# Reordering the opening of a fused attention and MLP kernel: first loads, small tables, first sixteenths, second chunk

## Chip, cores and metric

One core of a Trainium2 chip runs the kernel. The metric is the device time of one execution in microseconds (us). The engines have queues of their own and work in the order of their queues: PE (TensorE: matrix products; its weight loads are shown as PEld), DVE (VectorE), ACT (ScalarE), POOL (GpSimd) and SP (SyncE, which here only issues DMAs).

## The reference

Linear attention with decay over 4 batches, 8 heads, 768 positions and head size 64, in blocks of 64 with a carried state; then an MLP with a snake activation over the 3072 tokens.

```python
for b in range(nb):                       # blocks of 64 positions
    intra = np.einsum('bhic,bhjc->bhij', qb, kb) * Dmask[None]     # lam ** (i - j), i >= j
    intra = np.einsum('bhij,bhjd->bhid', intra, vb)
    inter = np.einsum('bhid,bhde->bhie', qb * lam_pow[None], kv_state)
    out[:, :, sl] = intra + inter
    kv_state = lam_block * kv_state + np.einsum('bhsd,bhse->bhde', kb * rev_pow, vb)
x = out.transpose(0, 2, 1, 3).reshape(B * S, H * D)                # 3072 x 512
h = x @ w_in                                                       # w_in 512 x 2048
g = h + np.sin(alpha * h) ** 2 / (alpha + 1e-09)
return g @ w_out                                                   # w_out 2048 x 512
```

Inputs and output are float32; the products run in bfloat16.

## The kernel before

The positions are cut into six chunks of 128. A chunk's attention over the four batches gives one group g of 512 tokens (128 of each batch), held as `xt[g]`: 128 partitions x 4 parts of the model dimension x 512 tokens, where batch b fills columns 128 b to 128 b + 127. A unit u = 4 t + b is batch b of chunk t.

The MLP goes by groups. Its hidden dimension of 2048 is cut into sixteen columns of 128, the sixteenths f. `hidden(g, f)` does four products of 512 columns on PE (line 400), then ACT takes the Sin (403) and, for most f, the Square (406); `finish(g, f)` on DVE adds that to h (413; for even f below 8 in group 0 it also squares, 412). `project(g, n)` does a quarter of an output tile (428). The order on every engine is written by hand: the loop at line 597 runs group g, and in its sixteenth i it places `hidden(g, i)`, the attention of chunk g + 1 as listed by `slots(g)` (541), a projection, `finish(g, i)`, and from `feed(g)` (574) the work of POOL and SP. PE, ACT and DVE each take their part of that list in that order.

Attention of one unit in chunks 0 and 1: `transposes` (221, 224) turns k and q on PE with an identity into one bank of PSUM, ACT copies the result (227, QKT); `scores` (235) makes the products of k and q in the bank `pf`, DVE multiplies them by the decay mask `Cmask` (243, STm); `intra_mm` (283) and `inter_mm` (291) make the output, `copy_x` (297) writes it to `xt`. In chunk 0 there is no carried state, and `first_out` (466, 470) does the output. `part_fo(uf, uo)` does the output of unit uo and the scores of uf in between. `part_k` (254, 261) makes the sums of the state, `state_put` (269) and `state_decay` (275) put them in place on POOL. Chunks 2 to 5 go by pairs of batches, with other tables (`NEp`, `Rpair`, `trip`, made in `tables_of_pairs`) and DMA transposes on SP.

Banks of PSUM go by tags: `pf`, `po`, `pqk`, `ops`, `h0`, `h1`, `h2` hold one thing at a time. The first nine sixteenths of group 0 take the banks of `FIRST`, later ones h0, h1, h2 in turn. The transposes of chunk 1's units use pqk, po, pqk, ops; the first projection needs ops.

Loads: k and q of batch 0 in chunk 0 come over SP's queue as float32 (`kraw`, `qraw`) and are cast by DVE (451, 458). Everything else is issued by POOL (line 100; chunks 2 on also at 96; w_in at 106, w_out at 110), which casts to bfloat16 on the way, in the order written: k and q of batch 1, v of batch 0, the rest of chunk 0, w_in in five pieces, chunk 1 in halves of two batches. The kdec products of POOL (214) stand among the last of these.

The opening (479 to 520) is chunk 0's attention, ahead of group 0. `spin(n)` puts n products without use on PE, as filling; `pcol` holds -1 - p, 127 - p and, in columns 2 and 3, the exponents of the pair tables, each made by iota on POOL; `pos_row` holds 1 to 128 in every row. `iden` and `idf` are identities made by POOL, `tri` the triangle of the mask.

Of the kernel before, what the change touches and what calls it, by code (L numbers as in the profile page):

```python
# [7 lines left out]

ALU = mybir.AluOpType
ACTF = mybir.ActivationFunctionType  # L10
FP32 = mybir.dt.float32
BF16 = mybir.dt.bfloat16
# [3 lines left out]
def kernel(  # L16
# [11 lines left out]
    nc = tc.nc  # L28
    P = nc.NUM_PARTITIONS

    B, H, S, D = q.shape
    T = 128
    NT = S // T
    HP = H // 2
    DM, DFF = moe_w_in.shape
    NDC = DM // P
# [40 lines left out]
    def new_chunk(t):  # L77
        for d, nm in ((qn, "qn"), (kn, "kn"), (vn, "vn")):
            d[t] = qkvp.tile([P, B, H, D], BF16, name=nm)
# [8 lines left out]
    def load(t, i, b0, b1):  # L88
        dst, src = KQV[i]
        if i != 1 and t >= 2:  # L90


            for c in range(b0 // 2, b1 // 2):
                for n in range(2):
                    t0 = t * T + c * D
                    nc.gpsimd.dma_start(  # L96
                        out=dst[t][n * D:(n + 1) * D, 2 * c:2 * c + 2, :, :].rearrange("p b h e -> p (b h) e"),
                        in_=src[2 * n:2 * n + 2, :, t0:t0 + D, :].rearrange("b h p e -> p (b h) e"))
            return
        nc.gpsimd.dma_start(  # L100
            out=dst[t][:, b0:b1, :, :].rearrange("p b h e -> p (b h) e"),
            in_=src[b0:b1, :, t * T:(t + 1) * T, :].rearrange("b h p e -> p (b h) e"))
# [6 lines left out]
    def load_w_out(i):  # L109
# [1 line left out]
                            in_=moe_w_out[i * 512:(i + 1) * 512, :].rearrange("(f p) d -> p f d", p=P))  # L111


    pcol = consts.tile([P, 4], FP32, name="pcol")
    nc.gpsimd.iota(out=pcol[:, 0:1], pattern=[[0, 1]], base=-1, channel_multiplier=-1,
                   allow_small_or_imprecise_dtypes=True)
    nc.gpsimd.iota(out=pcol[:, 1:2], pattern=[[0, 1]], base=T - 1, channel_multiplier=-1,
                   allow_small_or_imprecise_dtypes=True)
    new_chunk(0)
    load(0, 0, 1, 2)  # L120
    load(0, 1, 1, 2)
    iden = consts.tile([P, P], BF16, name="iden")
    make_identity(nc, iden[:])
    fill = consts.tile([P, 512], BF16, name="fill")
    nc.vector.memset(fill[:], 1.0)  # L125
    tri = consts.tile([P, T], FP32, name="tri")
    nc.vector.memset(tri[:], 1.0)
    nc.gpsimd.affine_select(out=tri[:], in_=tri[:], pattern=[[1, T]], compare_op=ALU.is_ge,
                            fill=0.0, base=0, channel_multiplier=-1)
    pos_row = consts.tile([P, T], FP32, name="pos_row")  # L130
    nc.gpsimd.iota(out=pos_row[:], pattern=[[1, T]], base=1, channel_multiplier=0,
                   allow_small_or_imprecise_dtypes=True)
    load(0, 2, 0, 1)
    for b in range(2, B):
        for i, bi in ((0, b), (1, b), (2, b - 1)):
            load(0, i, bi, bi + 1)
    load(0, 2, B - 1, B)
    for r in range(2):
        for c in range(2):
            nc.gpsimd.iota(out=pcol[r * D:(r + 1) * D, 2 + c:3 + c], pattern=[[0, 1]], base=-1 - D * c,  # L140
                           channel_multiplier=-1, allow_small_or_imprecise_dtypes=True)
    idf = consts.tile([NFC, NFC], FP32, name="idf")
    make_identity(nc, idf[:])
    for i in range(4):
        load_w_in(i)
    new_chunk(1)
    load(1, 0, 0, 2)
    load(1, 1, 0, 2)
    load_w_in(4)

    kv = [consts.tile([P, HP, 2, D], BF16, name=f"kv{b}") for b in range(B)]
    for b in range(B):
        nc.vector.memset(kv[b][:], 0.0)


    lnlam = consts.tile([P, H], FP32, name="lnlam")
# [17 lines left out]
    Cmask1 = consts.tile([P, 2, HP, D], FP32, name="Cmask1")  # L174
    Rpair = consts.tile([P, 2, H], FP32, name="Rpair")

    def powers_of_pairs():
        for c in range(2):
            nc.scalar.activation(out=NEp[:, c], in_=lnlam[:].rearrange("p (hp hd) -> p hd hp", hd=2),
                                 func=ACTF.Exp, scale=pcol[:, 2 + c:3 + c])  # L180

    def tables_of_pairs():

        lo, hi = slice(0, D), slice(D, P)
        nc.sync.dma_start(out=Rpair[hi, 0, :], in_=Rtok[lo, :])
        nc.sync.dma_start(out=Rpair[lo, 1, :], in_=Rtok[hi, :])
        nc.gpsimd.tensor_copy(out=Rpair[lo, 0, :], in_=Rtok[lo, :])
        nc.gpsimd.tensor_copy(out=Rpair[hi, 1, :], in_=Rtok[hi, :])
        nc.gpsimd.tensor_copy(out=trip[lo, :], in_=tri[lo, :])
        nc.gpsimd.memset(trip[hi, :], 1.0)  # L190
        nc.gpsimd.affine_select(out=trip[hi, :], in_=trip[hi, :], pattern=[[1, T]], compare_op=ALU.is_ge,
                                fill=0.0, base=0, channel_multiplier=-1)
        for c, C in enumerate((Cmask, Cmask1)):
            n = T - D * c
            nc.gpsimd.tensor_tensor(out=C[:], in0=trip[:, 0:n].unsqueeze(1).unsqueeze(1).broadcast_to([P, 2, HP, n]),
                                    in1=NEp[:, c].unsqueeze(3).broadcast_to([P, 2, HP, n]), op=ALU.mult)
# [195 lines left out]
    def h_tag(g, f):  # L392
        return f"h{(g * NFC + f) % 3}"

    def hidden(g, f):

        tag = FIRST[f] if g == 0 and f < len(FIRST) else h_tag(g, f)
        hps = psA.tile([P, GRP], FP32, name="hps", tag=tag)
        for c in range(NDC):
            nc.tensor.matmul(out=hps[:], lhsT=w_in_of[f][:, c, :],  # L400
                             rhs=xt[g][:, c, :], start=(c == 0), stop=(c == NDC - 1))
        s_sb = mlps.tile([P, GRP], BF16, name="s_sb")
        nc.scalar.activation(out=s_sb[:], in_=hps[:], func=ACTF.Sin, scale=alpha_sb[:, f:f + 1])  # L403
        s2 = mlps.tile([P, GRP], BF16, name="s2")
        if on_act(g, f):
            nc.scalar.activation(out=s2[:], in_=s_sb[:], func=ACTF.Square)  # L406
        hps_of[g, f] = (hps, s_sb, s2)
# [68 lines left out]
        for _ in range(n):  # L476
            nc.tensor.matmul(out=ps[:, 0:cols], lhsT=fill[:, 0:P], rhs=fill[:, 0:cols], start=True, stop=True)  # L477

    spin(9)
    for nm, src, tag in (("KT", kn, "pqk"), ("QT", qn, "ops")):  # L480
        X_ps = psA.tile([P, HP, T], BF16, name="X_ps", tag=tag)
        for hp in range(HP):
            nc.tensor.transpose(out=X_ps[:, hp, :], in_=src[0][:, 0, 2 * hp:2 * hp + 2, :], identity=iden[:])
        XT = firstp.tile([P, HP, T], BF16, name=nm)
        nc.scalar.copy(out=XT[:], in_=X_ps[:])
        st[0][nm] = XT[:]
        spin(3)
    scores(0)
    spin(1)
    transposes(1, "pqk")  # L490
    for hp in range(HP):
        nc.scalar.activation(out=Etab[:, hp, :], in_=pos_row[:], func=ACTF.Exp, scale=ln_hd[:, hp:hp + 1])
    spin(2)
    transposes(2, "ops")
    powers_of_pairs()
    warm = consts.tile([P, 1], FP32, name="warm")
    nc.scalar.activation(out=warm[:], in_=lnlam[:, 0:1], func=ACTF.Sin)
    spin(1)
    scores(1)
    spin(1)  # L500
    first_out(0, "po")
    spin(1)
    scores(2)
    a_ps = psA.tile([P, NFC], FP32, name="a_ps", tag="h2")
    nc.tensor.transpose(out=a_ps[:], in_=alpha_fp[:], identity=idf[:])
    transposes(3, "pqk")
    spin(2)
    first_out(1, "h1")
    alpha_sb = consts.tile([P, NFC], FP32, name="alpha_sb")
    nc.vector.tensor_copy(out=alpha_sb[:], in_=a_ps[:])  # L510
    r_sb = consts.tile([P, NFC], FP32, name="r_sb")
    nc.vector.reciprocal(out=r_sb[:], in_=alpha_sb[:])
    spin(2)
    scores(3, 2)
    spin(1)
    first_out(2, "po")
    spin(2)
    first_out(3, "h1", range(0, 2))
    first_out(3, "ops", range(2, 4))
    spin(3)  # L520


    def part_fo(uf, uo, bank="po"):
# [15 lines left out]
    def slots(g):  # L539

        u = [B * (g + 1) + b for b in range(B)]
        T_, FO = transposes, part_fo
        if g == 0:
            return {}, {3: [(part_k, (0, 1), "pf")], 6: [(part_k, (2, 3), "pf")],
                    7: [(T_, u[0])], 8: [(T_, u[1], "po")], 9: [(FO, u[0], None)],
                    11: [(FO, u[1], u[0]), (copy_x, u[0])], 12: [(T_, u[2])],
                    13: [(FO, None, u[1]), (T_, u[3], "ops"), (copy_x, u[1])], 14: [(FO, u[2], None)]}, {}

        p, q_ = (u[0], u[2]), (u[1], u[3])
        pre, at, post = {}, {}, {}  # L550
        if g == 1:
            at = {4: [(part_k, (4, 6), h_tag(1, 5))], 6: [(part_k, (5, 7), h_tag(1, 7))]}
        for us, s0, s1 in ((p, 9, 11), (q_, 13, 15)) if g == 1 else ((p, 5, 8), (q_, 10, 13)):

            early = g == 1 and us == q_
            scores_ = [(pair_scores, us, h_tag(g, s0 + 1))]
            out_ = [(pair_out, us, h_tag(g, s1 + 1) if g < NT - 2 else None), (sum_state, us[0]), (copy_x, us[0])]
            rest = [(copy_x, us[1]), (sum_state, us[1])]
            if early:
                pre[s0] = scores_ + [(pair_mask, us)]  # L560
                pre[s1] = out_ + rest
            else:
                at[s0], post[s0] = scores_, [(pair_mask, us)]
                at[s1], post[s1] = out_, rest
        return pre, at, post
# [102 lines left out]
```

## Time and profile before

| what | us |
|---|---|
| three runs | 215.27, 217.73, 215.68 |
| median | 215.68 |
| the profiled execution's own time | 217.63 |
| its span, first to last instruction | 215.70 |

| engine | busy us | share of the span |
|---|---|---|
| PE | 206.7 | 96% |
| ACT | 147.3 | 68% |
| DVE | 124.3 | 58% |
| POOL | 107.2 | 50% |

By place: the opening runs to 18.5 us, when group 0's first sixteenth starts on PE; sixteenth 15 of group 0 starts at 41.9, the first projection at 42.76, group 1 at 47.97. The matrix products of the MLP (lines 400 and 428) are on the chain of work that ended last for 71% of the span. The profile's page cuts the span into 40 slices; each digit is a share in tenths, and PEclk is the clock that PE was granted:

```profile
PE   7889986999999999999999999999999999999994
POOL 8999999896999799607479316210000000000000
PEclk9999999799999999999999999999999999999999
DMA  5999999999999999991995993990210101111022
```

A line of the timeline holds the start, the busy time, the engine, the line of the code, the operation with output and inputs, how many, and in brackets how long the engine had been idle and what ended that. Lines of several instructions have been merged, so that the busy time is that of all of them.

### The profile page before, as it was taken

The page shows a single profiled execution, that of the slowest core. Times are in us where ns is not written, and L with a number is a line of the kernel's source. Part 1 is how long each engine was busy: PE and PEld are TensorE (multiplying, and loading weights), DVE is VectorE, ACT ScalarE, POOL GpSimd, SP SyncE. Part 2 cuts the span into 40 slices and gives each one's busy share as a digit, 9 for nine tenths or more (in the row PEclk, how much of TensorE's full clock was granted, in tenths as well). Part 3 has the DMA queues.
Part 4 walks back from the last instruction along what each step waited for, and adds up shares of the span by engine and source line. Part 5 has one row for each costly group of instructions (what it writes and reads, how often), then busy time and mean ns, then how long its engine had stood idle before and what let it go on. Part 6 is the DMA issues. An engine that isn't in the chain of part 4 may idle for free.

```text
span 215.7 us, 4606 instructions
## 1 busy us (share of the span) xinstructions
PE 206.7 (96%) x1856; PEld 99.8 (46%) x1856; DVE 124.3 (58%) x191; ACT 147.3 (68%) x236; POOL 107.2 (50%) x155
## 2 busy tenths in 40 slices
PE   7889986999999999999999999999999999999994
PEld 2444443444444554454544454544454544444453
DVE  4576988472557784577664568654766644444300
ACT  5583897827776667975758785768767679788531
POOL 8999999896999799607479316210000000000000
PEclk9999999799999999999999999999999999999999
DMA  5999999999999999991995993990210101111022
GB/s 103 150 145 174 175 176 175 208 183 152 169 197 163 148 172 112 146 146 51 140 181 50 196 122 26 175 146 22 78 49 2 52 0 52 47 53 49 0 97 97
DMA packets 100214, 24.69 MB, mean 114 GB/s; under 512 B 92369, under 2 KB 97249, under 8 KB 100193
## 3 DMA queue, kind: packets, MB, share of 16 engines
q0 software_dynamic: 77280, 13.37, 80.3%
q1 hardware_dynamic: 22912, 11.03, 23.3%
q8 instruction: 14, 0.23, 0.5%
q14 instruction: 8, 0.06, 0.1%
HBM read 27.28 MB, written 6.29 MB: 156 GB/s over the span
## 4 chain that ended last, share of the span: by engine, by line
PE 81%; POOL 11%; DMA 5%; issue 1%; ACT 0%; POOLq 0%; ACTq 0%
PE ops L428 37%; PE hps L400 34%; DMA qn<-in_q_dram 5%; POOL vn L100 2%; POOL kn L100 2%; PE O_ps L371 2%; POOL kdec L214 2%; POOL qn L100 2%; POOL w_in L106 2%; PE hps L442 2%; PE O_ps L365 1%; PE F_ps L330 1%; PE KVA_ps L356 1%; PE O_ps L283 1%; PE O_ps L291 1%
## 5 line engine op out<-in xcount | busy, mean ns | idle before, releaser
L413 DVE SCALAR_TENSOR_TENSOR gall<-s,r_sb,hps 128x512 bf16<-128x512 bf16 x96 | 71.3, 746 | 62.1 <-ACT s L406 61.7
L400 PE MATMUL hps<-xt,w_in 128*128 128x512 bf16 x384 | 98.5, 382 | 0.1
L403 ACT ACTIVATE s_sb<-hps,alpha_sb 128x512 bf16<-128x512 f32 x96 | 65.8, 687 | 47.5 <-PE hps L400 47.5
L428 PE MATMUL ops<-w_out,gall 128*128 128x512 bf16 x368 | 93.1, 379 | 0.0
L406 ACT ACTIVATE s<-s_sb 128x512 bf16<-128x512 bf16 x92 | 57.9, 630 | 3.0
L400 PEld LDWEIGHTS <-w_in 128*128 128x128 bf16 x384 | 36.9, 98 | 44.7 <-issue 2.4
L428 PEld LDWEIGHTS <-gall 128*128 128x128 bf16 x368 | 34.9, 98 | 39.7
L269 POOL CAST kv<-kvs 64x256 bf16<-64x256 f32 x40 | 16.1, 402 | 30.4 <-PE O_ps L371 22.4
L297 DVE TENSOR_TENSOR xt<-O_ps,Etab 128x512 bf16<-128x512 f32 x20 | 13.7, 687 | 6.8 <-PE O_ps L291 3.5
L433 ACT COPY o_sb<-ops 128x512 f32<-128x512 f32 x23 | 13.1, 571 | 6.0 <-PE ops L428 6.0
L96 POOL DMA_DIRECT2D kn<-in_k_dram x16 | 13.3, 850 | 0.0
L96 POOL DMA_DIRECT2D vn<-in_v_dram x16 | 13.2, 845 | 0.0
L100 POOL DMA_DIRECT2D qn<-in_q_dram x10 | 12.8, 1278 | 0.7 <-DMA w_out<-in_moe_w_out_dram 0.7
L477 PE MATMUL hps<-fill 128*128 128x512 bf16 x31 | 10.9, 459 | 1.5 <-DVE fill L125 1.5
L306 POOL TENSOR_TENSOR kdec<-kn,Rpair 128x1024 bf16<-128x1024 bf16 x6 | 11.4, 1910 | 1.6 <-DMA kn<-in_k_dram 1.6
L243 DVE TENSOR_TENSOR STm<-F_ps,Cmask 128x1024 bf16<-128x1024 f32 (+1 forms) x9 | 9.8, 1095 | 3.5 <-PE F_ps L235 3.5
L275 POOL TENSOR_TENSOR kvd<-kvs,L 128x256 f32<-128x256 f32 x16 | 9.8, 615 | 1.0
L341 DVE TENSOR_TENSOR STm<-F_ps,Cmask 128x1024 bf16<-128x1024 f32 x8 | 9.7, 1217 | 0.0
L227 ACT COPY QKT<-QK_ps 128x1024 bf16<-128x1024 bf16 x7 | 7.0, 1004 | 2.7 <-PE QK_ps L224 2.7
L214 POOL TENSOR_TENSOR kdec<-kn,Rtok 128x512 bf16<-128x512 bf16 x8 | 8.5, 1106 | 0.1
L338 DVE TENSOR_TENSOR STm<-G_ps,Cmask 128x256 bf16<-128x256 f32 x16 | 6.0, 419 | 0.6
L100 POOL DMA_DIRECT2D vn<-in_v_dram x6 | 6.0, 1012 | 0.0
(83 smaller groups left out, 116.1 us busy)
## 6 DMA issues: line engine op xcount, KB each, us to landing
out_dram<-o_sb SPq DMA_DIRECT2D x23, 256.0 KB, 2.2
vn<-in_v_dram POOLq DMA_DIRECT2D x20, 128.0 KB, 4.9
kn<-in_k_dram POOLq DMA_DIRECT2D x19, 128.0 KB, 5.8
w_out<-in_moe_w_out_dram POOLq DMA_DIRECT2D x4, 512.0 KB, 14.0
w_in<-in_moe_w_in_dram POOLq DMA_DIRECT2D x3, 512.0 KB, 9.8
qn<-in_q_dram POOLq DMA_DIRECT2D x3, 512.0 KB, 9.1
qn<-in_q_dram POOLq DMA_DIRECT2D x4, 256.0 KB, 11.7
w_in<-in_moe_w_in_dram POOLq DMA_DIRECT2D x2, 256.0 KB, 5.7
```

What stands on the lines that cost most here:

```text
L96: nc.gpsimd.dma_start(out=dst[t][n * D:(n + 1) * D, 2 * c:2 * c + 2, :, :].rearrange("p b h e -> p (b h) e"), in_=src[2 * n:2 * n + 2, :, ...
L100: nc.gpsimd.dma_start(out=dst[t][:, b0:b1, :, :].rearrange("p b h e -> p (b h) e"), in_=src[b0:b1, :, t * T:(t + 1) * T, :].rearrange("b h ...
L214: nc.gpsimd.tensor_tensor(out=kdec[:], in0=kn[t][:, b, :, :], in1=head_bc(Rtok), op=ALU.mult)
L269: nc.gpsimd.tensor_copy(out=kv[b][s, :, hd, :], in_=kvs[u][s, :, :])
L297: nc.vector.tensor_tensor(out=xt[t][:, :, b * T:(b + 1) * T], in0=st[u]["O_ps"], in1=Etab[:], op=ALU.mult)
L306: nc.gpsimd.tensor_tensor(out=kdec[:], in0=kn[t][:, b::2, :, :], in1=Rpair[:].unsqueeze(3).broadcast_to([P, 2, H, D]), op=ALU.mult)
L400: nc.tensor.matmul(out=hps[:], lhsT=w_in_of[f][:, c, :], rhs=xt[g][:, c, :], start=(c == 0), stop=(c == NDC - 1))
L403: nc.scalar.activation(out=s_sb[:], in_=hps[:], func=ACTF.Sin, scale=alpha_sb[:, f:f + 1])
L406: nc.scalar.activation(out=s2[:], in_=s_sb[:], func=ACTF.Square)
L413: nc.vector.scalar_tensor_tensor(out=gall[g][:, f, :], in0=s2[:], scalar=r_sb[:, f:f + 1], in1=hps[:], op0=ALU.mult, op1=ALU.add)
L428: nc.tensor.matmul(out=ops[:], lhsT=gall[g][:, f, m * P:(m + 1) * P], rhs=w_out_sb[part][:, f % 4, :], start=(f == 0), stop=(f == NFC - 1))
L433: nc.scalar.copy(out=o_sb[:], in_=ops[:])
```

## The change

- POOL issues the loads of k and q of batch 1 first, and the iotas `pcol` and `pos_row` follow. `pcol` keeps two columns; the four iotas of columns 2 and 3 go.
- `iden`, `tri` and `idf` are made by DVE from `pos_row` and `pcol`. The memsets of `kv` stand ahead of them in the code.
- `NEp`, which ACT made with two Exps, is put together of `NE`: one half by two DMAs on SP, the other by two copies on POOL. The DMAs of `Rpair` now stand at the top level, behind those.
- In the opening the order on PE changes: the transposes of batch 1 come ahead of scores 0, the alpha transpose and its reciprocal come early, scores 1 comes ahead of the transposes of batch 2, both outputs of batches 0 and 1 ahead of scores 2, and batch 3 is transposed in two halves (`half_T`) with a copy each. The Exps of `Etab` stand behind the copy of batch 1, the warming Sin behind scores 2.
- `hidden` can begin a sixteenth with the first 256 columns (batches 0 and 1) and do the other 256 later. The opening ends with such a beginning of sixteenths 0 and 1 of group 0.
- In group 0 the list of chunk 1's attention moves by one sixteenth: transposes of the four units in sixteenths 8, 9, 13, 14 in place of 7, 8, 12, 13, the rest with them. `feed` is as before.

```diff
+    new_chunk(0)
+    load(0, 0, 1, 2)
+    load(0, 1, 1, 2)
+    pcol = consts.tile([P, 2], FP32, name="pcol")
     nc.gpsimd.iota(out=pcol[:, 0:1], pattern=[[0, 1]], base=-1, channel_multiplier=-1,
...
+    nc.vector.tensor_scalar(out=iden[:], in0=pos_row[:], scalar1=pcol[:, 0:1], scalar2=0.0,
+                            op0=ALU.add, op1=ALU.is_equal)
     tri = consts.tile([P, T], FP32, name="tri")
+    nc.vector.tensor_scalar(out=tri[:], in0=pos_row[:], scalar1=pcol[:, 0:1], scalar2=0.0,
+                            op0=ALU.add, op1=ALU.is_ge)
+    idf = consts.tile([NFC, NFC], FP32, name="idf")
+    nc.vector.tensor_copy(out=idf[:], in_=iden[0:NFC, 0:NFC])
...
-    for r in range(2):
-        for c in range(2):
-            nc.gpsimd.iota(out=pcol[r * D:(r + 1) * D, 2 + c:3 + c], pattern=[[0, 1]], base=-1 - D * c,
-                           channel_multiplier=-1, allow_small_or_imprecise_dtypes=True)
-    idf = consts.tile([NFC, NFC], FP32, name="idf")
-    make_identity(nc, idf[:])
...
+    nc.sync.dma_start(out=NEp[hi, 0], in_=NE[lo])
+    nc.sync.dma_start(out=NEp[lo, 1], in_=NE[hi])
+    nc.sync.dma_start(out=Rpair[hi, 0, :], in_=Rtok[lo, :])
+    nc.sync.dma_start(out=Rpair[lo, 1, :], in_=Rtok[hi, :])
...
+        nc.gpsimd.tensor_copy(out=NEp[lo, 0], in_=NE[lo])
+        nc.gpsimd.tensor_copy(out=NEp[hi, 1], in_=NE[hi])
...
+    def hidden(g, f, start_only=False):
+        parts = [slice(0, GRP)]
+        if (g, f) in begun:
+            hps, parts = begun.pop((g, f)), [slice(GRP // 2, GRP)]
+        else:
+            hps = psA.tile([P, GRP], FP32, name="hps", tag=tag)
+        if start_only:
+            begun[g, f], parts = hps, [slice(0, GRP // 2)]
+        for w in parts:
+            for c in range(NDC):
+                nc.tensor.matmul(out=hps[:, w], lhsT=w_in_of[f][:, c, :],
+                                 rhs=xt[g][:, c, w], start=(c == 0), stop=(c == NDC - 1))
+        if start_only:
+            return
...
+    spin(9)
+    half_T(0, "KT", "pqk")
+    spin(3)
+    half_T(0, "QT", "ops")
+    spin(1)
+    transposes(1, "po")
+    spin(1)
     scores(0)
...
     spin(2)
+    scores(1)
+    spin(1)
+    transposes(2, "pqk")
+    spin(1)
+    first_out(0, "po")
+    spin(1)
+    first_out(1, "h1")
+    spin(1)
+    scores(2)
...
+    half_T(3, "KT", "ops")
+    spin(1)
+    half_T(3, "QT", "h2")
+    spin(1)
+    first_out(2, "po")
     scores(3, 2)
+    spin(3)
     first_out(3, "h1", range(0, 2))
     first_out(3, "ops", range(2, 4))
-    spin(3)
+    hidden(0, 0, True)
+    hidden(0, 1, True)
...
-                    7: [(T_, u[0])], 8: [(T_, u[1], "po")], 9: [(FO, u[0], None)],
-                    11: [(FO, u[1], u[0]), (copy_x, u[0])], 12: [(T_, u[2])],
-                    13: [(FO, None, u[1]), (T_, u[3], "ops"), (copy_x, u[1])], 14: [(FO, u[2], None)]}, {}
+                    8: [(T_, u[0])], 9: [(T_, u[1], "po")], 10: [(FO, u[0], None)],
+                    12: [(FO, u[1], u[0]), (copy_x, u[0])], 13: [(T_, u[2])],
+                    14: [(FO, None, u[1]), (T_, u[3], "ops"), (copy_x, u[1])], 15: [(FO, u[2], None)]}, {}
```

More of the change, by code (lines that the diff above doesn't have):

```diff
@@ L6 @@
 from concourse._compat import with_exitstack
-from concourse.masks import make_identity
 ALU = mybir.AluOpType
@@ L111, in load_w_out @@
                             in_=moe_w_out[i * 512:(i + 1) * 512, :].rearrange("(f p) d -> p f d", p=P))
-    pcol = consts.tile([P, 4], FP32, name="pcol")
+    new_chunk(0)
+    load(0, 0, 1, 2)
+    load(0, 1, 1, 2)
+    pcol = consts.tile([P, 2], FP32, name="pcol")
     nc.gpsimd.iota(out=pcol[:, 0:1], pattern=[[0, 1]], base=-1, channel_multiplier=-1,
+                   allow_small_or_imprecise_dtypes=True)
+    pos_row = consts.tile([P, T], FP32, name="pos_row")
+    nc.gpsimd.iota(out=pos_row[:], pattern=[[1, T]], base=1, channel_multiplier=0,
                    allow_small_or_imprecise_dtypes=True)
@@ L118 @@
                    allow_small_or_imprecise_dtypes=True)
[L119 to L123, printed above, removed]
     fill = consts.tile([P, 512], BF16, name="fill")
     nc.vector.memset(fill[:], 1.0)
-    tri = consts.tile([P, T], FP32, name="tri")
[L127 to L132, printed above, removed]
+    kv = [consts.tile([P, HP, 2, D], BF16, name=f"kv{b}") for b in range(B)]
+    for b in range(B):
+        nc.vector.memset(kv[b][:], 0.0)
+    iden = consts.tile([P, P], BF16, name="iden")
+    nc.vector.tensor_scalar(out=iden[:], in0=pos_row[:], scalar1=pcol[:, 0:1], scalar2=0.0,
+                            op0=ALU.add, op1=ALU.is_equal)
+    tri = consts.tile([P, T], FP32, name="tri")
+    nc.vector.tensor_scalar(out=tri[:], in0=pos_row[:], scalar1=pcol[:, 0:1], scalar2=0.0,
+                            op0=ALU.add, op1=ALU.is_ge)
+    idf = consts.tile([NFC, NFC], FP32, name="idf")
+    nc.vector.tensor_copy(out=idf[:], in_=iden[0:NFC, 0:NFC])
     load(0, 2, 0, 1)
@@ L149 @@
     load_w_in(4)
-    kv = [consts.tile([P, HP, 2, D], BF16, name=f"kv{b}") for b in range(B)]
-    for b in range(B):
-        nc.vector.memset(kv[b][:], 0.0)
     lnlam = consts.tile([P, H], FP32, name="lnlam")
@@ L175 @@
     Rpair = consts.tile([P, 2, H], FP32, name="Rpair")
[L177 to L180, printed above, removed]
+    lo, hi = slice(0, D), slice(D, P)
+    nc.sync.dma_start(out=NEp[hi, 0], in_=NE[lo])
+    nc.sync.dma_start(out=NEp[lo, 1], in_=NE[hi])
+    nc.sync.dma_start(out=Rpair[hi, 0, :], in_=Rtok[lo, :])
+    nc.sync.dma_start(out=Rpair[lo, 1, :], in_=Rtok[hi, :])
     def tables_of_pairs():
-        lo, hi = slice(0, D), slice(D, P)
-        nc.sync.dma_start(out=Rpair[hi, 0, :], in_=Rtok[lo, :])
-        nc.sync.dma_start(out=Rpair[lo, 1, :], in_=Rtok[hi, :])
+        nc.gpsimd.tensor_copy(out=NEp[lo, 0], in_=NE[lo])
+        nc.gpsimd.tensor_copy(out=NEp[hi, 1], in_=NE[hi])
         nc.gpsimd.tensor_copy(out=Rpair[lo, 0, :], in_=Rtok[lo, :])
@@ L393, in h_tag @@
         return f"h{(g * NFC + f) % 3}"
-    def hidden(g, f):
+    begun = {}
+    def hidden(g, f, start_only=False):
         tag = FIRST[f] if g == 0 and f < len(FIRST) else h_tag(g, f)
[L398 to L401, printed above, removed]
+        parts = [slice(0, GRP)]
[11 more added lines that the diff above has]
+            return
         s_sb = mlps.tile([P, GRP], BF16, name="s_sb")
@@ L477, in spin, with half_T @@
             nc.tensor.matmul(out=ps[:, 0:cols], lhsT=fill[:, 0:P], rhs=fill[:, 0:cols], start=True, stop=True)
-    spin(9)
-    for nm, src, tag in (("KT", kn, "pqk"), ("QT", qn, "ops")):
+    def half_T(u, nm, tag):
+        src = {"KT": kn, "QT": qn}[nm]
         X_ps = psA.tile([P, HP, T], BF16, name="X_ps", tag=tag)
         for hp in range(HP):
-            nc.tensor.transpose(out=X_ps[:, hp, :], in_=src[0][:, 0, 2 * hp:2 * hp + 2, :], identity=iden[:])
+            nc.tensor.transpose(out=X_ps[:, hp, :], in_=src[0][:, u, 2 * hp:2 * hp + 2, :], identity=iden[:])
         XT = firstp.tile([P, HP, T], BF16, name=nm)
         nc.scalar.copy(out=XT[:], in_=X_ps[:])
-        st[0][nm] = XT[:]
-        spin(3)
+        st[u][nm] = XT[:]
+    spin(9)
[5 more added lines that the diff above has]
+    spin(1)
     scores(0)
-    spin(1)
-    transposes(1, "pqk")
+    a_ps = psA.tile([P, NFC], FP32, name="a_ps", tag="h2")
+    nc.tensor.transpose(out=a_ps[:], in_=alpha_fp[:], identity=idf[:])
     for hp in range(HP):
         nc.scalar.activation(out=Etab[:, hp, :], in_=pos_row[:], func=ACTF.Exp, scale=ln_hd[:, hp:hp + 1])
[L493 to L508, printed above, removed]
     alpha_sb = consts.tile([P, NFC], FP32, name="alpha_sb")
@@ L513 @@
     spin(2)
-    scores(3, 2)
+    scores(1)
[7 more added lines that the diff above has]
+    scores(2)
+    warm = consts.tile([P, 1], FP32, name="warm")
+    nc.scalar.activation(out=warm[:], in_=lnlam[:, 0:1], func=ACTF.Sin)
+    spin(1)
+    half_T(3, "KT", "ops")
+    spin(1)
+    half_T(3, "QT", "h2")
     spin(1)
     first_out(2, "po")
-    spin(2)
+    scores(3, 2)
+    spin(3)
     first_out(3, "h1", range(0, 2))
     first_out(3, "ops", range(2, 4))
-    spin(3)
+    hidden(0, 0, True)
+    hidden(0, 1, True)
     def part_fo(uf, uo, bank="po"):
```

## The prediction

> **What bounds the kernel now.** I read the chain that ended last first: where the end is decided.
>
> ```profile
> 18.42 4.25 POOL kdec L214 x4
> 22.67 1.18 POOL vn L100
> 23.85 1.12 POOL kn L100
> 24.97 11.80 DMA qn<-in_q_dram
> 36.81 0.57 PE QK_ps L224 x4
> 37.38 1.71 PE hps L400 x4
> ```
>
> Columns: start, length, what. POOL's queue, full from 1.9 us, leads to the issue at 24.97 of q of chunk 1, batches 2 and 3. It lands 11.80 us later, at 36.77, and its transposes start at once. After that the chain is all but PE. Then PE's timeline around it:
>
> ```profile
> 33.41 1.02 PE L400 MATMUL hps<-xt,w_in 128*128 128x512 bf16 x4
> 35.09 0.40 PE L221 MATMUL QK_ps<-iden,kn 128*128 128x128 bf16 x4 [0.66 <-DMA kn<-in_k_dram]
> 36.81 0.57 PE L224 MATMUL QK_ps<-iden,qn 128*128 128x128 bf16 x4 [1.32 <-DMA qn<-in_q_dram]
> 37.18 1.91 PE L400 MATMUL hps<-xt,w_in 128*128 128x512 bf16 x4
> ```
>
> PE waits 1.98 us (0.78 more stood at 27.7, before the q of batches 0 and 1), and the sixteenth after it takes 1.7 us where others take 0.86. Busy time by stretch (length; PE, PEld, DVE, ACT, POOL; clock, DMA share, GB/s) tells why:
>
> ```profile
> 33.50:36.90 3.40, 1.42 (x12) 0.51 (x10) 3.05 (x5) 2.73 (x5) 3.31 (x5) 1.00 2.18 171
> 38.00:39.00 1.00, 1.00 (x3) 0.15 (x1) 0.00 (x0) 0.43 (x1) 1.00 (x2) 0.50 1.26 213
> ```
>
> PE was busy 1.42 of 3.40 us, then had half its clock from 36.9 to 40.4. Half of 3.4 us is 1.7 us lost. ACT's timeline shows that little slack lies behind:
>
> ```profile
> 35.66 0.63 ACT L406 ACTIVATE s<-s_sb 128x512 bf16<-128x512 bf16 x1
> 37.42 1.01 ACT L227 COPY QKT<-QK_ps 128x1024 bf16<-128x1024 bf16 x1 [1.13 <-PE QK_ps L224]
> 39.13 0.69 ACT L403 ACTIVATE s_sb<-hps,alpha_sb 128x512 bf16<-128x512 f32 x1 [0.69 <-PE hps L400]
> ```
>
> ACT was busy until 36.29: had q been there, PE would soon have met ACT.
>
> **Part 1, POOL and the loads.** POOL loses identity and triangle (3.35 to 4.17, 0.82 us), four iotas (11.31 to 11.93, 0.62) and the small identity (to 12.33, 0.40): 1.84 us. Two iotas and `pos_row` only move behind the first two issues. So k and q of batch 1 issue up to 0.52 us earlier (1.43 to 0.91), the other loads of chunk 0 about 0.82, w_in and chunk 1 about 1.84; kdec, the state casts and w_out, queued behind them, move too. What lands earlier by L is less sure, for the DMA engines have a backlog:
>
> ```profile
> qn<-in_q_dram POOLq DMA_DIRECT2D x1, 256.0 KB, 11.8
> 14.00:15.00 1.00, 1.00 (x18) 0.58 (x15) 0.98 (x1) 0.99 (x3) 1.00 (x2) 1.00 1.37 128
> 17.00:18.00 1.00, 1.00 (x12) 0.49 (x11) 1.00 (x3) 0.00 (x0) 1.00 (x2) 1.00 1.10 109
> 18.00:20.00 2.00, 1.94 (x10) 0.83 (x9) 0.70 (x3) 0.33 (x1) 2.00 (x3) 1.00 1.16 183
> ```
>
> From 14 to 18 us they moved 128, 151, 197 and 109 GB/s against some 188 from 18 to 22: (4 x 188 - 585) / 188 = 0.9 us of moving was lost behind POOL's gap. At the start 0.5 to 0.8 us is regained, 3 to 5 us being far from full. L is thus 1.3 to 1.84, and its bounds are 0 and 1.84. I take 1.6: q at 35.2.
>
> The Trainium skill's "Trainium Kernel Development and Optimization", section Key Constraints, says that DMAs of all issuing queues share the same 16 engines, so that a change of issuer saves only issue time. Read against this change it would make L 0; the dip in GB/s above says that issue time did cost moving.
>
> **Part 2, identity, triangle and tables.** DVE makes three small tiles (nearest row: its 128x128 memset, 0.17 us), 0.5 us in all, after `pos_row` at about 3.5 us. That ends near 4.1, and DVE had nothing from 2.7 to 4.13 and the transposes need kn's cast at 5.47; without that cover the cost is 0.5. ACT loses two Exps (0.49 us) in the opening, where it idles later. Two more small DMAs go on SP's queue (0.59 us of issue each) with the two of Rpair, which stood there at 6.0 already; behind them comes a transpose at 50.16. POOL gets two copies of 0.18 us at 46.8, before a kdec that waits 1.62 us for its load: hidden. Nothing for all of it.
>
> **Part 3, the opening.** DVE's order decides. From qn's cast (ends 7.25, if q still lands at 6.73; software packets that start 0.5 to 0.8 us sooner could hold it up by as much) PE does QT (0.40), a fill, the transposes of batch 1 (0.45; k and q at 6.7 and 7.7), a fill, scores 0 from 8.65. Then DVE: mask 0 1.22, to 10.3; alpha and reciprocal 0.4; mask 1 1.22, to 11.95 (before: 13.25, as transposes 2 waited for q until 11.04 ahead of scores 1); two xt of 0.67 with 0.25 of waiting, 13.5; mask 2, 14.7; a wait of 0.5 for PE; xt 2, 15.85; mask 3, 17.1; both halves of xt 3, 17.85. Before: 18.70. PE meanwhile does the first two batches of sixteenths 0 and 1: 8 products of 256 columns at 0.11, 0.86 us, from 17.4 to 18.25, with w_in there at about 16.3 (if still at 17.8, as before, 0.4 later). The second halves end at 19.1; before, 18.61 + 2 x 0.86 = 20.33. ACT's first Sin starts at 18.25 + 0.43 + 0.20 = 18.9 (before 19.67, the 0.20 being its lag behind PE).
>
> **Part 4, group 0 a sixteenth later.** ACT's need by its spacings: a Sin 0.56; Sin and Square 1.26; a QKT copy 0.90. 4 x (0.56 + 1.26) + 8 x 1.26 + 4 x 0.90 = 20.96 us. Before, it took 24.64 (19.67 to 44.31), 2.87 of it in listed waits. In the new order PE asks for the late q at 34.0, behind sixteenth 13; ACT is busy with Sin and Square 13 until 36.0, so q may land until 35.6 (0.22 transposes, 0.2 lag) at no cost. The first q of the chunk, 27.66 less L, comes before PE asks for it at 26.7 behind sixteenth 8. I find 0.5 of other waits: PE's two groups of state products (0.37 each) and sixteenth 8, whose bank waits for the finish of sixteenth 4 (DVE, behind its square beside kdec, 1.38 us in the row). So ACT ends near 18.9 + 20.96 + 0.5 = 40.4, and the last QKT copy 1.26 sooner, 39.1.
>
> What is late next: that copy frees the bank of the first projection, which now follows sixteenth 15 at once (before, the copy was done at 41.80 and the projection ran at 42.76). On DVE the mask of batch 2 now queues behind the finish of sixteenth 14, itself behind a Square: it ends at 40.2, against a projection's end at 40.05, so the output products wait 0.15. From first projection to first product of group 1 was 47.97 - 42.76 = 5.21. New: 39.1 + 5.21 + 0.15 = 44.46, a gain of 3.5 us. w_out's first quarter landed at 40.3 and is needed at 39.1, which holds for L over 1.2. Later PE has no idle time of note (42.00 busy of 42.00 from 50 to 92), so the 3.5 us reach the end.
>
> **The sum.** The profiled execution took 217.63 (span 215.70, 1.93 around it): 217.63 - 3.5 = 214.1. But it is 1.95 above the median of 215.68, like the run of 217.73; I take it that the half clock, 1.6 us of the way to 47.97, was missing from the other two. Against those only 1.9 is left: 215.5 - 1.9 = 213.6. I take 213.9.
>
> The Trainium skill's "TensorE: Matmul & The Clock Gate", Part 1, puts the gate down to an idle window of some 3.4 us that runs free. The trace's longest wait was 1.32 us and still cost the clock; by the rule alone it would not have, and the median's whole gain would be PE's waits.
>
> **Rivals.**
> - A: the engines, not POOL, time the loads (L about 0.3; the 11.80 us of latency speaks for it, the dip against). Then q lands at 36.5, ACT stalls 0.9 and w_out holds the first projection at 40.0: 213.9 + 1.0 = 214.9, with the clock kept, as one sixteenth less stands behind the wait.
> - B, slower: the half clock strikes behind that wait. With L under 0.3 PE waits from 34.0 to 36.8, and sixteenths 14 and 15 with their attention (3.1 us) run at half clock: 37.2 + 3.1 + 1.75 = 42.0, 0.35 until the projection's bank and mask are ready, then 5.21: 47.6. That is 217.63 - 0.4 = 217.2, above the median. It decides where PE is under about 1.5 of 3.4 us busy; for it speaks the row of 1.42, against it that 2.41 of 3.40 (10.0 to 13.4) kept the clock, and the new order has some 2.1.
> - C: ACT's spacing packs better and the finish of sixteenth 4 is not late (0.65 less), and w_in and q let the opening end 0.5 earlier: 212.7.
> - D: the opening does not do what it says: the q of batch 0, sharing engines with earlier software packets, lands 0.8 later and DVE's chain shifts as a whole: 214.7.
>
> **How the numbers follow.** Mine 0.52, A 0.13, B 0.10, C 0.17, D 0.08. A measurement here tells about 1% from no change: under 213.5 is faster, over 217.8 slower. My own case spreads 213.1 to 214.8, about 0.4 of it under 213.5; with C that is 0.38, and 0.04 for an L over 1.84 through better packing of the queue: 0.42. Slower by over 1% needs B with D or with a second half-clock stretch: 0.08. The rest, 0.50, is within. The range takes in C, A, D and half of B: 212.4 to 216.3.
>
> **What would show it.** Right: POOL's first issue near 0.9 and w_in's near 10.5; q of batches 2 and 3 before 35.6; no wait of over 1.3 us on PE before the transposes of sixteenth 13; clock 1.00 from 30 to 50; ACT without idle time from 20 to 39; first product of group 1 near 44.5. Wrong: a DVE end of the opening after 18.3 (D), a q after 36.3 (A), a clock of 0.50 (B), or ACT idle in group 0, which says that PE or DVE bounds it, and that the loads were not all.

## The result and the profile after

| kernel | median us | runs | lowest to highest |
|---|---|---|---|
| before | 215.95 | 20 | 215.27 to 217.73 |
| after | 214.75 | 20 | 214.31 to 215.14 |

The ratio of after to before is 0.9934, with a 95% interval of 0.9917 to 0.9952: about 0.7% faster, 1.2 us by the medians. The runs of after fall into two groups of ten, 214.31 to 214.55 and 214.95 to 215.14, and the median lies in the gap between them. The profiled execution took 214.55 us with a span of 212.8, against 217.63 and 215.7: 3.08 us less. The two gains differ mainly because the profiled execution of before is one of the few that had the half clock: of 83 runs of the kernel before, taken beside the comparisons below, seven had a mean clock of 0.990 to 0.992. Six of those took 217.4 to 218.2 us, one 216.3; of the other 76 only one was above 217.

The chain that ended last in the kernel after, around the same q (start, length, what):

```profile
21.05 1.17 POOL vn L99
22.22 1.12 POOL kn L99
23.34 12.19 DMA qn<-in_q_dram
35.58 0.40 PE QK_ps L220 x4
35.97 0.86 PE hps L406 x4
...
38.82 0.35 PE F_ps L231 x8
39.19 1.24 DVE STm L239
40.47 0.41 PE O_ps L279 x8
```

The same q is still on the chain. It is issued 1.63 us earlier (23.34 against 24.97) but lands only 1.24 us earlier (35.53 against 36.77), since its latency grew from 11.80 to 12.19. Behind it the mask of batch 2 has come onto the chain. PE's timeline and then that of ACT, both of the kernel after:

```profile
33.31 1.02 PE L406 MATMUL hps<-xt,w_in 128*128 128x512 bf16 x4
34.17 0.39 PE L217 MATMUL QK_ps<-iden,kn 128*128 128x128 bf16 x4
35.58 0.40 PE L220 MATMUL QK_ps<-iden,qn 128*128 128x128 bf16 x4 [1.02 <-DMA qn<-in_q_dram]
35.81 1.03 PE L406 MATMUL hps<-xt,w_in 128*128 128x512 bf16 x4
...
39.29 1.02 PE L436 MATMUL ops<-w_out,gall 128*128 128x512 bf16 x4
40.47 0.41 PE L279 MATMUL O_ps<-STm,vn 128*64 128x128 bf16 x8 [0.15 <-DVE STm L239]
...
44.72 1.02 PE L406 MATMUL hps<-xt,w_in 128*128 128x512 bf16 x4
```

```profile
35.56 0.63 ACT L414 ACTIVATE s<-s_sb 128x512 bf16<-128x512 bf16 x1
36.09 0.99 ACT L223 COPY QKT<-QK_ps 128x1024 bf16<-128x1024 bf16 x1
36.99 0.69 ACT L411 ACTIVATE s_sb<-hps,alpha_sb 128x512 bf16<-128x512 f32 x1
```

PE waits 1.02 us for this q where before it waited 1.98 us for its k and q, and sixteenth 14 behind it takes its usual 0.86. ACT goes from Square 13 to the copy of that q's transposes without idle time: q and ACT arrive together. Group 1 starts at 44.72 instead of 47.97; its first line in PE's timeline of before, and from the chain the last 32 narrow products, before and after:

```profile
47.97 1.02 PE L400 MATMUL hps<-xt,w_in 128*128 128x512 bf16 x4
209.09 3.51 PE hps L442 x32
205.83 3.51 PE hps L450 x32
```

Busy time by stretch of the kernel after (length; PE, PEld, DVE, ACT, POOL; clock, DMA share, GB/s), for the idle stretch of before and for 14 to 18 us:

```profile
33.50:36.90 3.40, 2.38 (x20) 1.17 (x20) 3.15 (x5) 3.34 (x6) 3.40 (x5) 1.00 1.75 190
14.00:18.00 4.00, 3.36 (x40) 2.01 (x38) 3.44 (x6) 1.24 (x4) 3.94 (x5) 1.00 1.48 198
```

PE was busy 2.38 us of 3.40 where it had been 1.42, and the clock stayed at 1.00. The DMA engines moved 198 GB/s from 14 to 18 us; before, the same stretch reads:

```profile
14.00:18.00 4.00, 4.00 (x49) 1.91 (x47) 3.71 (x8) 1.46 (x3) 4.00 (x5) 1.00 1.30 146
```

From group 1's start to the last 32 narrow products, 161.12 us passed before (47.97 to 209.09) and 161.11 after (44.72 to 205.83): what is won by then stays won. But from the last copy of ACT to the end of the span it takes 3.0 us before and 3.4 after (spans are given to 0.1 us). That is why the span gained only 2.9 us where the start of group 1 gained 3.25.

### The profile page after: what moved, and what is told of

Same layout as the page of the kernel before. It is cut to its first block, busy times and chain, and to the rows that moved or that the text cites. A ratio compares the mean times of both kernels' runs of the same rounds, so it can differ in the third digit from the quotient of the medians.

```text
span 212.8 us, 4607 instructions
## 1 busy us (share of the span) xinstructions
PE 203.8 (96%) x1859; PEld 99.9 (47%) x1859; DVE 124.6 (59%) x193; ACT 146.7 (69%) x235; POOL 106.0 (50%) x148
## 4 chain that ended last, share of the span: by engine, by line
PE 81%; POOL 10%; DMA 6%; issue 1%; DVE 1%; ACT 0%; POOLq 0%; ACTq 0%
PE ops L436 37%; PE hps L406 34%; DMA qn<-in_q_dram 6%; POOL kn L99 2%; POOL vn L99 2%; PE O_ps L367 2%; POOL kdec L210 2%; POOL w_in L105 2%; PE hps L450 2%; PE O_ps L361 1%; POOL qn L99 1%; PE F_ps L326 1%; PE KVA_ps L352 1%; DVE STm L239 1%; PE O_ps L279 1%
## 5 line engine op out<-in xcount | busy, mean ns | idle before, releaser
L406 PE MATMUL hps<-xt,w_in 128*128 128x512 bf16 (+1 forms) x392 | 97.6, 375 | 0.0
L406 PEld LDWEIGHTS <-w_in 128*128 128x128 bf16 x392 | 37.4, 98 | 43.5 <-issue 1.7
L485 PE MATMUL hps<-fill 128*128 128x512 bf16 x26 | 9.9, 476 | 1.5 <-DVE fill L125 1.5
L223 ACT COPY QKT<-QK_ps 128x1024 bf16<-128x1024 bf16 x6 | 6.0, 1000 | 1.0 <-PE QK_ps L220 0.8
```

The source lines that it names most:

```text
L406: nc.tensor.matmul(out=hps[:, w], lhsT=w_in_of[f][:, c, :], rhs=xt[g][:, c, w], start=(c == 0), stop=(c == NDC - 1))
```

## The experiments

Theory Q: the landing of chunk 1's last q, with ACT close behind it, sets the start of group 1, and the loads' change is what moved it. Rivals: the opening's order carries the gain (O), or the later attention is only a price (P). The three parts were run alone and in pairs, against the kernel before on the same chip.

**One part alone.** Each is the kernel before with the lines of the change that belong to that part.

loads:

```diff
+    new_chunk(0)
+    load(0, 0, 1, 2)
+    load(0, 1, 1, 2)
+    nc.vector.tensor_scalar(out=iden[:], in0=pos_row[:], scalar1=pcol[:, 0:1], scalar2=0.0,
+                            op0=ALU.add, op1=ALU.is_equal)
...
+    nc.sync.dma_start(out=NEp[hi, 0], in_=NE[lo])
```

> The kernel before with the new loads and tables alone (order of the opening and places of chunk 1's attention as before). Theory Q (the arrival of chunk 1's last q, and PE's work behind it, set the start of group 1): q of batches 2 and 3 lands at about 35.5 instead of 36.8, the start of group 1 moves by the same 1.2 us; about 214.8 against 215.95. Rival O (the opening's order carries the gain): the loads alone give at most the 0.5 us of the first issues; 215.5. In both the half clock behind the wait may come as before.

opening:

```diff
+    transposes(1, "po")
+    spin(1)
     scores(0)
...
+    hidden(0, 0, True)
+    hidden(0, 1, True)
```

> The kernel before with the new order of the opening and the two begun sixteenths alone; alpha's transpose stays behind scores 2, because its identity is still made late. Theory Q: sixteenth 1 ends about 0.7 us earlier, but q still lands at 36.8, PE only waits longer for it, and the half clock is no rarer: 215.9, no change within 0.3. Rival O: the 1 us of the opening goes through to the end: 214.9.

slots:

```diff
-                    7: [(T_, u[0])], 8: [(T_, u[1], "po")], 9: [(FO, u[0], None)],
+                    8: [(T_, u[0])], 9: [(T_, u[1], "po")], 10: [(FO, u[0], None)],
```

> The kernel before with chunk 1's attention a sixteenth later alone. Theory Q: q lands at 36.8, sixteenth 13 now stands ahead of the wait, and behind it PE needs the 9.1 us to group 1 that it takes after the change (44.72 - 35.58): group 1 at 45.9 instead of 46.4 with the clock kept and 48.0 without, and the clock is kept: about 215.4, and a smaller spread. Rival P (the shift has only its price, the mask of batch 2 behind the finish of sixteenth 14): 216.2 to 216.5.

**Pairs.** The same pieces, two at a time.

> New loads and later attention, with the opening's order as before. Theory Q: q lands at 35.5, PE's 9.1 us behind it as in the kernel after, but ACT starts some 0.6 us later than there and stands in front: between 214.8 and 215.2. Rival O: without the opening's order most of the gain is gone: 215.5.

> The kernel after with chunk 1's attention where it was before. Theory Q: PE asks for q a sixteenth earlier, at about 33.2, and waits over 2 us for it; sixteenth 13 (0.86 us) stands behind the wait, but the mask of batch 2 no longer queues behind a finish (0.15 to 0.3 back): 0.5 later than after, 215.2, and in some runs the half clock comes, 1.5 more. Rival P (the shift is only a price): 214.5.

> The kernel after with loads and tables as before. Theory Q: q lands at 36.8, 1.2 us later than after, and all behind it with it: 215.4 to 216.0 (more where the longer wait brings the half clock). Rival O: nearly the whole gain stays, 214.8.

The last column is the start of group 1 in each kernel's profile; before had 47.97, with the half clock.

| parts | median us | ratio to before, 95% interval | group 1, us |
|---|---|---|---|
| loads | 214.85 | 0.9939 (0.9919 to 0.9959) | 44.99 |
| opening | 216.17 | 1.0016 (0.9989 to 1.0043) | 46.83 |
| slots | 215.90 | 0.9999 (0.9969 to 1.0028) | 45.96 |
| loads, opening | 214.93 | 0.9934 (0.9907 to 0.9961) | 45.23 |
| loads, slots | 215.51 | 0.9969 (0.9943 to 0.9996) | 45.63 |
| opening, slots | 215.67 | 0.9977 (0.9950 to 1.0003) | 45.82 |
| all three (after) | 214.75 | 0.9934 (0.9917 to 0.9952) | 44.72 |

The loads alone give the whole gain, and neither other part gives any alone: Q holds against O. For the slots alone Q expected 215.4 and a smaller spread. Neither showed, though group 1 started at 45.96 as expected (45.9): the median is that of before, and one of 12 runs took 217.86 with a clock of 0.991. Two of the 12 of the opening had 0.989 and 0.990 (218.03 and 218.47). Opening with slots came as expected. In the profile of the loads alone PE's timeline shows q as in the kernel after:

```profile
35.39 0.40 PE L221 MATMUL QK_ps<-iden,qn 128*128 128x128 bf16 x4 [1.07 <-DMA qn<-in_q_dram]
```

Why the opening is worth nothing by itself, PE's timeline of that kernel shows; the first sixteenths were ready to begin, and their weights were not there:

```profile
17.84 0.30 PE L479 MATMUL O_ps<-STm,vn 128*64 128x128 bf16 x4 [0.30 <-DVE STm L244]
19.59 3.65 PE L411 MATMUL hps<-xt,w_in 128*128 128x256 bf16 x24 [1.45 <-DMA w_in<-in_moe_w_in_dram]
```

The later attention has a price, as P says, where ACT starts late. With loads and slots but the old opening (ACT's first Sin at 19.65, against 19.01 after), the timeline of PE no longer waits for q but for others, three times for over 0.5 us:

```profile
32.23 1.02 PE L397 MATMUL hps<-xt,w_in 128*128 128x512 bf16 x4 [0.55 <-DVE gall L410]
...
37.34 0.41 PE L280 MATMUL O_ps<-STm,vn 128*64 128x128 bf16 x8 [0.64 <-DVE xt L294]
40.36 1.02 PE L425 MATMUL ops<-w_out,gall 128*128 128x512 bf16 x4 [0.63 <-ACT QKT L224]
```

The last is the wait that the prediction named as late next: the first projection's bank, freed by ACT's last QKT copy. So the slots cost 0.66 us on top of the loads (215.51 - 214.85), and the opening's earlier ACT pays that back. ACT's last QKT copy shows it. The first line is from loads with slots, the second from the kernel of the next experiment, which has the new opening: there the first Sin comes at 18.64, and the same wait of 0.63 us ends at 39.35.

```profile
39.31 0.99 ACT L224 COPY QKT<-QK_ps 128x1024 bf16<-128x1024 bf16 x1
38.30 0.99 ACT L223 COPY QKT<-QK_ps 128x1024 bf16<-128x1024 bf16 x1
```

From the one kernel to the other the first Sin, the last copy and the first projection all come 1.01 us earlier, and in both the chain that ended last goes through ACT's queue here and not through this q. With the loads alone it goes through q (issued at 23.13, there 12.21 us later). The expected 214.8 to 215.2 for this pair and 215.2 for loads with opening were both off by 0.3.

**Sixteenths 0 and 1 not begun in halves** (the kernel after without these lines):

```diff
-    hidden(0, 0, True)
-    hidden(0, 1, True)
```

> The kernel after without the beginning of sixteenths 0 and 1 in halves. Theory Q with ACT just behind it: ACT's first Sin hardly moves (it comes 0.1 us later), the second Sin 0.35, and since ACT runs without a gap until the copy behind q, group 1 comes 0.2 to 0.35 later: 215.0 against 214.75. Rival O: the 0.5 to 0.86 us come back in full: 215.3 to 215.6. If q alone binds: 214.75.

Measured 214.44 (0.9934, 0.9913 to 0.9955): not slower than after, against theory and rival, and in the lower of after's two groups; one of the 12 runs took 216.22, with a clock of 0.990. The number is nearest to "q alone binds", but q is not what binds here. ACT's first Sin came earlier, at 18.64 against 19.01, since sixteenth 0 is whole before sixteenth 1 starts. And q landed in time for its transposes at 34.84. It was then ACT that PE waited for, as the timeline of this kernel shows:

```profile
34.84 0.40 PE L220 MATMUL QK_ps<-iden,qn 128*128 128x128 bf16 x4 [0.23 <-DMA qn<-in_q_dram]
...
39.35 1.02 PE L436 MATMUL ops<-w_out,gall 128*128 128x512 bf16 x4 [0.63 <-ACT QKT L223]
...
44.62 1.02 PE L406 MATMUL hps<-xt,w_in 128*128 128x512 bf16 x4
```

A q that comes 0.74 us earlier moves group 1 by 0.10 (44.72 to 44.62): ACT stands right behind q, and its last QKT copy starts no earlier than after (38.30 against 38.25).

**The wait of before, filled** (products without use around the transposes of the third unit, in sixteenth 12):

```diff
+        if filler:
+            spin(3, tag="ops")
         for hp in range(HP):
             nc.tensor.transpose(out=QK_ps[:, 1, hp, :],
...
+        if filler:
+            spin(5, tag="ops")
```

> The kernel before with products without use put into the wait for chunk 1's third k and q: three ahead of the transposes of k and five between those of k and q, into the free bank ops. Theory H (the clock falls because PE stood nearly idle for some 3.4 us, and that makes part of the spread of 215.27 to 217.73 of the kernel before): the clock stays at 1.00 from 30 to 50 us, group 1 starts at about 46.4, the slowest times go, the median falls by 0.2 to 0.5. Without H: the clock falls as before or the times only gain the 0.1 to 0.2 us that the products cost.

The median is 215.85 against 215.89 beside it: no gain that can be told. But none of its 12 runs had a mean clock under 0.999, and the slowest took 216.61; beside it four of 35 runs of before had 0.991 or 0.992 and took 217.56 to 218.07. Four in 35 is too rare for twelve runs to settle it by count alone. The stretch from 30 to 50 us, first of before and then of this kernel, shows the clock itself:

```profile
30.00:50.00 20.00, 17.99 (x148) 8.88 (x147) 12.82 (x16) 12.88 (x20) 18.72 (x27) 0.91 1.84 183
```

```profile
30.00:50.00 20.00, 19.98 (x165) 9.80 (x164) 13.74 (x17) 14.34 (x22) 19.30 (x28) 1.00 1.84 183
```

Group 1 started at 45.91 with the wait filled (46.4 expected; q came some 0.4 us earlier here). The half clock is thus a cost of some runs, about 2 us each, and not of the median run. That the idle wait is its only cause is not shown: a clock of 0.989 to 0.992 also came in three of 24 runs of the two kernels without halves (one above, two below), whose profiles have no wait of PE over 0.63 us from 20 us to group 1. Where it fell in those runs no trace shows.

**The loads' change cut in two.** In loads_mid the four iotas and the small identity leave POOL, and with them the two Exps of `NEp` give way to DMAs and copies; in loads_first only the first issues move ahead, and identity and triangle go to DVE.

```diff
-    for r in range(2):
-        for c in range(2):
-            nc.gpsimd.iota(out=pcol[r * D:(r + 1) * D, 2 + c:3 + c], pattern=[[0, 1]], base=-1 - D * c,
-                           channel_multiplier=-1, allow_small_or_imprecise_dtypes=True)
```

> The kernel before with one part of the loads' change: the four iotas and the small identity leave POOL, 1.02 us between the last v of chunk 0 and w_in; first loads, identity and triangle as before. Theory E (POOL's gap starves the DMA engines from 14 to 18 us, 0.9 us of moving): q lands 0.8 to 1.0 earlier, 215.0 to 215.2. Rival B (the engines' backlog takes it up): 215.9.

> The kernel before with the other part: first loads ahead of the iotas, identity and triangle on DVE, 0.7 us of POOL before the first v; the four iotas and the small identity stay on POOL and the Exps on ACT. Theory E: the engines start to fill 0.3 to 0.6 us earlier and q with them: 215.4 to 215.6. Rival B: 215.9. If issue alone sets the landing: 215.25, and 214.95 in the run with the middle part.

loads_mid took 215.03 (0.9955, 0.9937 to 0.9973), as theory E expected. loads_first took 214.58 (0.9931, 0.9914 to 0.9949), 0.8 to 1.0 us under what E expected of it, under both rivals too, and no worse than both parts together. The transposes of q started at 35.51 and 35.30, against 35.39 with both parts: either part brings the whole 1.3 to 1.5 us (36.81 before), and they do not add. Nor does the landing follow the issue of that q, which came at 23.62, 24.28 and 23.13. From loads_first:

```profile
35.30 0.40 PE L225 MATMUL QK_ps<-iden,qn 128*128 128x128 bf16 x4 [0.87 <-DMA qn<-in_q_dram]
```

In all profiles with the old loads this start lies between 36.25 and 37.24, in all with new ones (either part or both) that wait for q between 34.84 and 35.64. Theory E does not stand as it was put: loads_first keeps POOL's gap, as POOL's timeline shows, and the engines have no dip all the same; the second fence has the stretches of that kernel:

```profile
8.88 1.81 POOL L100 DMA_DIRECT2D vn<-in_v_dram  x2
10.63 0.58 POOL L145 IOTA pcol<- 64x1 f32 x4
...
11.66 1.54 POOL L106 DMA_DIRECT2D w_in<-in_moe_w_in_dram  x2
```

```profile
14.00:15.00 1.00, 1.00 (x16) 0.58 (x16) 1.00 (x1) 0.99 (x3) 1.00 (x2) 1.00 1.60 192
17.00:18.00 1.00, 1.00 (x12) 0.45 (x11) 1.00 (x3) 0.00 (x0) 1.00 (x2) 1.00 1.20 198
```

Before, these two read 128 and 109 GB/s. With w_in issued at 12.33 to 12.55 all profiles show the dip (125 to 146 GB/s from 14 to 18); issued at 11.66 or earlier, all show 195 to 200. It looks like a point between, past which w_in comes too late for the end of chunk 0's packets; no run here moved the issue finely enough to show that this is the cause.

**The two late waits taken away.** Scores of batch 2 with the output of batch 1, and the projections of the first two tiles swapped, so that the bank pqk, free early, goes first:

```diff
-                    14: [(FO, None, u[1]), (T_, u[3], "ops"), (copy_x, u[1])], 15: [(FO, u[2], None)]}, {}
+                    14: [(FO, u[2], u[1]), (T_, u[3], "ops"), (copy_x, u[1])]}, {}
...
-            project(0, 0)
+            project(0, 1)
             part_fo(7, 6)
             copy_x(6)
-            project(0, 1)
+            project(0, 0)
```

> The kernel after with two places changed: the scores of batch 2 stand with the output of batch 1 in sixteenth 14, so that their mask comes ahead of the finish of sixteenth 14 on DVE; and the first quarter of output tile 1 (bank pqk, free early) comes ahead of that of tile 0 (bank ops, which waits for the last QKT copy of ACT). Theory Q+ACT (that copy and that mask stand on the path by 0.14 and 0.15 to 0.4 us): the output products start at 40.05 instead of 40.47; 0.3 to 0.4 less than after: 214.4. If only q binds: 214.75 as after.

> The same two places changed, and sixteenths 0 and 1 not begun in halves. There the first projection waited 0.63 us for ACT's last QKT copy. Theory Q+ACT: 0.4 to 0.5 less than the 214.44 without halves: 214.0. If ACT's pace alone binds and the swap only moves the wait: 214.4.

In the profiles the output products start at 40.10 and 40.03 and group 1 at 44.35 and 44.29: 0.37 and 0.33 earlier than without, as expected. The times hardly follow: 214.63 (six runs, 214.03 to 214.78) and 214.42 (twelve, 214.10 to 216.22, two of them with a clock of 0.989 and 0.992). These are the lowest single times of the study, but the medians, 0.12 under after and 0.02 under the kernel without halves, tell no gain. In the first, 0.3 us was lost again between group 1's start and the last products (161.40 us, where all other profiles have 161.1). The chain of that kernel shows where: v of chunk 2 landed at 66.50, and a group of products that needs it took 0.73 us from 66.13 on, where after it takes 0.45. That v was issued behind a kdec that waited for k of chunk 2 (issued at 37.01, there 14.84 us later), so a load is next in line again:

```profile
58.32 8.18 DMA vn<-in_v_dram
66.50 0.04 issue
66.55 0.31 PE KVA_ps L352 x14
```

## Why the prediction was right, and where it was off

The direction was right, and so was the path: the late q of chunk 1, with ACT right behind it. 213.9 was forecast and 214.75 measured, inside a range of 3.9 us; from the median of 215.68 that the forecast had, it promised 1.8 us, and by the medians 1.2 came. By its steps:

- *POOL's queue.* w_in issued at 10.61 (some 10.5 forecast), the last q 1.63 us earlier (1.84). The first issue came at 1.30, not 0.9: POOL has an idle time of 0.79 us ahead of it, so most of the 0.52 was not to be had.
- *L, the landing.* Taken at 1.6, measured 1.24: a latency of 12.19 in place of 11.80 took 0.4 back. The Trainium skill's "Trainium Kernel Development and Optimization", section Key Constraints, says that issuing from several engines at once saves only issue time. That does not make L 0, as the prediction read it: the change takes work from ahead of POOL's issues, and 1.24 us came of it. The reason given, moving lost behind POOL's gap, does not hold as it stands: the dip also goes with the gap left in place (loads_first). That L came within 0.4 of the forecast is thus in part luck, and what sets it stays open.
- *Tables.* Priced at nothing. DVE made its three small tiles from 3.69 to 4.63, 0.94 us instead of 0.5, and the casts of k and q of batch 0 ended some 0.2 us later than before.
- *The opening.* DVE ended at 18.0 (17.85 forecast, 18.70 before), ACT's first Sin started at 19.01 (18.9).
- *Group 0 a sixteenth later.* Forecast: q may land until 35.6 before ACT feels it, the last QKT copy and the mask of batch 2 are late next. All three showed: q at 35.53 and ACT without idle time from 25.58 to the copy, the mask's wait of 0.15, the copy's wait as 0.63 where ACT is later or q earlier. That the 0.15 came out exactly is luck: the chain has the mask behind its scores, which ended 0.05 us after the finish that it was to queue behind. Group 1 started at 44.72 (44.46).
- *The sum.* 217.63 - 3.5 = 214.1 by its own execution, measured 214.55. The missing 0.45 is 0.26 at the start of group 1 and some 0.4 at the span's end, which no step had, less some 0.2 around the span. Of the 0.26, 0.11 stood already at ACT's first Sin and 0.19 at the first projection (39.29 against 39.1); the smaller L can have added little, since a q 0.74 us earlier moved group 1 by 0.10 (the kernel without halves).
- *The half clock.* That the median lacked it was right. The term that was mis-sized is "215.5 - 1.9 = 213.6": 215.5 was the mean of two low runs. The median of twenty is 215.95, and 217.63 - 215.95 = 1.68 is what the half clock was priced at (1.6 to 1.7). From it the same 1.9 leads to 214.05; of the 0.70 that remain, 0.45 is the sum's error above and 0.20 the distance of after's median from its profiled run.

Of the rivals, A (a late q, 214.9) lies nearest in time, but its L of about 0.3 and its stall of ACT did not show; B did not occur in 20 runs of after. What the prediction did not see is how little the parts other than the loads bring: by its sum the opening and the slots were needed, in the runs they cancel (214.85 with the loads alone, 214.75 with all three).

## What to carry to other kernels

Where one late load and an engine's queue arrive together, moving either alone pays only until it meets the other: look for the second in line before pricing a change, and test the parts alone, since here one of three did all the work. When a profiled execution is far from the median, find the stretch that makes the difference (here the granted clock) and take the gain from the run that the median stands for. A median of three runs is a poor base for a forecast of 1%.

## What the hardware showed unasked

- The end of the span. From ACT's last copy to the end it took 3.0 to 3.1 us in the six profiles in which ACT makes NEp (before, opening, slots, opening with slots, filled, loads_first), and 3.4 to 3.5 in the eight in which two DMAs of SP and two copies of POOL do. Before and after read thus, ACT's last line of each:

```profile
212.67 0.37 ACT L446 COPY o_sb<-hps 128x256 f32<-128x256 f32 x1 [1.37 <-PE hps L442]
```

```profile
209.40 0.37 ACT L454 COPY o_sb<-hps 128x256 f32<-128x256 f32 x1 [1.37 <-PE hps L450]
```

  The spans end at 215.7 and 212.8. Two small DMAs early on go with some 0.35 us at the very end; loads_first, which keeps the Exps, is 0.27 us under the loads with the DMAs. No run exchanged them alone, so that they are the cause is not shown.
- The same q, issued at 23.3 to 23.4 us, was there at 34.84 and 34.86 in the two kernels without halves and at 35.54 to 35.64 in the three with them. Whether that has to do with the two groups of after's runs stays open; its profiled run, 214.55, is of the lower group and has the later q.
- In the one traced execution that had it, the half clock came after a stretch in which PE was busy 1.42 of 3.40 us, with no single wait over 1.32 us. The Trainium skill's "TensorE: Matmul & The Clock Gate", Part 1, puts the half clock down to an idle window of some 3.4 us. This trace differs: the window before it was 42% busy. A stretch of after with 2.38 of 3.40 us busy kept the clock.
